# Gated transposing loads and a new step order in a fused attention and GELU kernel

## The chip, the cores and the metric

The kernel runs on one core of one Trainium2 chip. The metric is the device time of one execution in microseconds (us). A core has five engines that each work through their own list of instructions in order: TensorE (PE in the profile; PEld is its loading of weights), VectorE (DVE), ScalarE (ACT), GpSimd (POOL) and SyncE (SP). Transfers between the chip's main memory (DRAM) and the core are DMAs. An engine issues them, and they then run beside it; an instruction that needs the data waits for the landing.

## What is computed

The reference is a cross-covariance attention followed by a feed-forward layer with a tanh GELU. Cut to what matters:

```python
B, N, C = 4, 6080, 256                    # q, k, v: float32 [4, 6080, 256]
qn = q / norm(q over N);  kn = k / norm(k over N)
s = kn.transpose(0, 2, 1) @ qn / tau      # [4, 256, 256], one small matrix per batch
a = softmax(s over the last axis)
x = (v @ a).reshape(24320, 256)
h = x @ w_in                              # [24320, 2048]
g = 0.5 * h * (1 + tanh(sqrt(2 / pi) * (h + 0.044715 * h**3)))
out = g @ w_out                           # [24320, 256], float32
```

## The kernel before, in words

For each batch b the kernel folds the attention matrix into the first weight matrix: AW[b] = a @ w_in, of 256 by 2048. What is left per token is gelu(v @ AW[b]) @ w_out. The tokens of the four batches are cut into 25 blocks m = 0 to 24, of 1024 tokens in most cases, each in two halves t = 0 and 1 of 512 columns.

**Attention part.** q and k come in chunks of four rows of 128 tokens, cast to bf16 by DMAs that GpSimd issues (`load_one`, L243, steps `lq` and `lk`; four buffers each). TensorE adds up the matrix of k and q row by row (`gram_row`, L290, steps `r`, tile G), and the squares for the norms are made beside it (steps `z`, `d`, `f`). A short chain then makes AW of the next batch (`aw` and `ac` steps). Batch 0 is done ahead of everything else; batches 1 to 3 are spread among the blocks of the batch before.

**The v tiles.** A half block of v takes two DMAs. `cast_v` (L306, step `lv`, for instance `1:lv1` for block 1, half 1) lets GpSimd issue a load that casts 512 tokens from float32 to bf16 into a DRAM tile vb; there are five such buffers. `load_vt` (L319, step `lt`) lets SyncE issue a transposing DMA (DMA_TRANSPOSE) from vb into the tile vT, channels by tokens, with three buffers for whole blocks. The three first halves (block 0, and half 0 of block 1) are transposed by TensorE instead (steps `vp` and `vc`). SyncE also issues the output's stores (`store`, L771, steps `O`), four DMAs for each half block, in the same list.

**The block part.** The first product is done in two ways: plainly (steps `j`, L560, with the GELU in steps `J`) for some of the 16 feature groups, and for the others by a scheme with seven products in place of eight (steps `s..m1` to `s..m7`, L628, with sums of v tiles made by VectorE in steps `vs` and copies and GELUs around them). The second product is of the same kind (steps `M`, L739, of which TensorE has 1400 matmuls), with sums of g tiles by VectorE (steps `T`), and VectorE turns the result for the stores (steps `c11` to `c22`, L768).

**What sets the order.** All of this is one list, `ORDER` (from L962), of 4017 steps written out. A step's name is block:step or b-batch:step. The loop at the end of the kernel goes through it and issues each step's instructions, so that each engine gets its instructions in the order of this list; an engine waits only for the tiles that its next instruction needs.

**Gates.** `GATE[0]` (L518) always holds the last matmul that the list has issued in the steps `j`, `s..m`, `M` and `r`. `after(inst, gate)` (L92) makes an instruction wait for that matmul. Before the change, `step` and `block_step` (L895, L922) pass the gate to the cast loads alone: `lq`, `lk` and `lv`. Such a load is issued when TensorE has reached its place in the list. A transposing load has no gate: SyncE issues it as soon as its vb tile has landed, its vT buffer is free and what stands before it in SyncE's list is done.

Of the kernel before, what the change touches and what calls it, by code (L numbers as in the profile page):

```python
# [973 lines left out]
1:j21 2:lv1 1:s3m5 0:M5A b1:r1.2 1:vs1 2:lt0 b1:r1.3 1:s3y5 1:s4m1 1:s3m2 1:s3m6 1:J21 1:s4m5 b1:zk1
1:s3G0 0:M5B 1:s4y5 0:T2a 1:s3ap 0:T2b 1:s4cq b1:zq0 :pS4 0:M6A 1:s3m3 1:s4m2 1:s4m6 1:s4ap b1:r2.0
0:M6B 1:s3m7 1:s4G0 1:vs2 b1:r2.1 0:y5 1:s3G1 b1:r2.2 :pNA b1:lk4 1:j01 b1:zq1 1:s5m1 1:s4m3 0:ap
1:s4m7 1:s3ax 0:M7A 0:M3A 1:s3Gx 1:J01 0:T4a 0:M7B 1:s3m4 1:s4G1 1:s5cq b1:f1.1 b1:zq2 1:s4ax 1:s4m4
b1:r2.3 1:s4Gr 1:s5m5 0:M3B 1:s5m6 1:s3Gr b1:lq4 1:s5y5 1:s5m2 1:s6m5 1:s5G0 1:s4Gx b1:r3.0 b1:f0.1
1:s6m1 0:T4b 0:ax 0:c12 1:s5ap b1:f1.2 1:s6cq b1:dk2 0:M4A b1:r3.1 1:s5m7 1:j20 b1:r3.2 1:s5ax
1:s6y5 1:s5m3 b1:f2.1 b1:zk3 1:J20 1:s6m6 1:s6ap b1:lq5 1:s5G1 0:M4B 1:s5m4 b1:r3.3 0:c21 1:s7m5  # L980
1:s5Gx 1:s6m7 1:s6m2 1:s5Gr 1:s6ax 1:s7m1 1:s6G0 1:s7cq 1:s6m3 2:j00 1:s7y5 1:M1A 1:s6G1 1:s7m6
1:T3a b1:f1.3 b1:r4.0 1:s7ap 1:s6m4 b1:r4.1 2:J00 2:lt1 2:j20 b1:r4.2 1:s7m7 1:s7m2 1:s7m3 1:s6Gx
b1:lq8 0:O0 b1:zq3 3:lv1 1:T1a 2:J20 2:j10 1:s7G1 1:s7ax 1:M1B b1:f3.1 b1:lq7 1:T2a 2:J10 b1:dk4
1:s7m4 2:vs0 1:s7Gx 1:s7G0 1:s7Gr b1:r4.3 b1:r5.0 1:s6Gr b1:r5.1 1:M5A b1:r5.2 1:x1 2:j11 1:T3b
2:vs1 2:s2m1 1:T1b 2:j21 2:J11 2:J21 b1:zq4 b1:lk9 2:s2m5 1:M6A 1:M2A 1:M2B 2:s2cq b1:lq6 2:s2y5
b1:lk6 b1:zq5 2:s2m6 2:vs2 1:T2b 2:s2m2 2:s3m1 2:s2ap b1:lk7 1:M5B 2:s2m7 1:M6B b1:zk5 2:s2m3
b1:f3.2 2:s2G0 1:c11 4:lv1 1:y5 2:j01 3:lt0 2:s3cq 2:s2ax 3:lt1 2:s2m4 2:s2G1 1:ap 2:J01 2:s3m6
2:s3m2 2:s2Gr 2:s3m5 1:T4a 1:M3A b1:f5.1 2:s4m5 2:s3y5 2:s3G0 2:s4m1 2:s3ap b1:f3.3 0:c22 1:M3B
2:s4y5 2:s4cq b1:f3.4 2:s3m3 2:s3m7 b1:r5.3 2:s2Gx 2:s4m6 2:s3G1 2:s4m2 1:M7A 2:s4ap 2:s4G0 2:s3ax
b1:r6.0 2:s4m3 b1:r6.1 2:s5m5 2:s3m4 b1:zq6 1:T4b 2:j30 b1:lk8 2:s4G1 2:s3Gr b1:r6.2 3:j11 2:s3Gx  # L990
2:s4m7 2:s5y5 2:s5m1 1:M7B 1:c12 2:s4ax b1:r6.3 3:J11 2:s4m4 2:s5cq 2:J30 2:s6m1 2:s4Gr 2:s6cq
b1:r7.0 2:s4Gx 2:s5m2 b1:f4.1 1:ax 0:O1 b1:dk6 2:s5m6 1:M4A 2:s6m5 2:s5ap 2:s5G0 2:s5m7 b1:f5.2
5:lv0 2:s6y5 2:s6m2 2:s5ax 5:lv1 2:s5m3 2:s6m6 2:s6G0 1:M4B 1:c22 2:s5G1 2:j31 2:s5Gx b1:lq9 2:s7m1
2:s6ap 1:c21 2:s5m4 2:J31 b1:f5.3 2:s6m7 2:s5Gr 2:M1A 2:s7cq 2:T3a 2:s6m3 b1:f5.4 b1:zk7 b1:r7.1
2:s7m5 3:j30 2:s7m6 2:s6ax 2:M1B b1:r7.2 2:s6m4 b1:r7.3 2:s7y5 b1:lq11 2:s7ap 2:s6G1 3:J30 2:s6Gx
2:T1a 2:s7m7 2:s7m2 2:s7m3 3:j21 2:s7ax 2:x1 b1:f6.1 2:s6Gr b1:r8.0 2:M2A 2:s7m4 b1:r8.1 2:s7G1
3:J21 3:j00 2:T2a 2:s7G0 3:vs0 2:s7Gx 3:j01 b1:lk10 3:j10 b1:r8.2 b1:r8.3 2:s7Gr 2:T3b 3:s2m1 3:J01
b1:zq7 3:vs1 3:J10 2:M2B 3:s2cq 2:T1b 1:O1 2:M5A 3:s2m5 b1:lk11 3:J00 3:s2m2 3:s2y5 3:s2m6 3:s3m1
3:s2G0 b1:f7.1 2:M5B 2:M6A b1:zk9 3:s3cq 2:c11 3:vs2 3:s3m5 3:s2ap 2:y5 3:s3y5 3:s2m7 3:s2m3 b1:r9.0
2:T2b b1:lq10 3:s3m6 2:M6B 3:s2ax 3:s3ap 3:s2G1 b1:zq9 3:s2m4 3:j20 3:s2Gx 2:ap 2:T4a 3:s3m7 3:s3ax  # L1000
4:lt0 3:s3m2 3:s2Gr 3:s3m3 3:J20 3:s3G1 2:M7A 3:s4m1 3:s4cq 2:M3A 3:s3m4 3:s4m5 3:s3G0 3:s4m2 3:s3Gr
b1:f7.2 3:s4y5 2:M3B 3:s4G0 3:s5m1 b1:dk8 b1:r9.1 3:s4m6 2:T4b 3:s3Gx 5:lt0 2:c12 b2:lk0 5:lt1 3:j31
2:M7B 3:s5cq 3:s4ap 3:s4m7 3:J31 b1:f9.1 b1:f7.3 4:j10 b1:zq8 3:s5m2 3:s5m5 3:s5m6 4:J10 3:s4ax
3:s4m3 3:s4m4 3:s5G0 2:ax b1:f7.4 4:j00 3:s5y5 3:s5ap 2:M4A b1:r9.2 2:c22 4:J00 3:s4G1 3:s6m1 3:s4Gx
b1:f8.1 3:s5m3 b2:lq1 3:s6cq 3:s5m7 3:s5G1 3:s6m5 2:M4B 3:s6y5 3:s6m6 3:s4Gr b1:r9.3 3:s5ax 4:j30
2:c21 3:s5m4 b1:r10.0 3:s6m2 3:s6ap 3:s7m1 3:s6m7 b1:r10.1 3:s7m5 b1:r10.2 3:s6m3 b1:r10.3 3:s5Gx
4:J30 3:s6G0 b1:f9.2 3:s7cq 3:s6ax 4:lt1 3:s6m4 3:s7m2 3:s7y5 3:s7m6 4:j01 3:s6G1 3:s5Gr 3:s6Gr
3:T3a 4:j20 3:s7ap 4:j21 3:s7m3 3:T1a 3:s7m7 3:s6Gx 3:s7ax 3:M1A 4:J20 4:J21 3:T2a b1:f9.3 3:s7G0
b1:r11.0 3:s7m4 4:s3m1 b1:dk10 b1:r11.1 b1:r11.2 4:J01 3:s7G1 8:lv1 3:s7Gr 3:M1B b1:r11.3 4:s2m1
4:s3cq 3:x1 3:s7Gx 3:M5A 4:vs0 b1:gc b1:zq10 3:M6A b1:f9.4 4:s3m2 1:O0 4:vs1 4:s2m5 4:s2cq 4:s3G0  # L1010
6:lv1 4:s2y5 3:M2A 3:T3b 3:M2B 4:vs2 b1:zq11 6:lv0 4:s2m2 3:T1b 4:s3m5 3:c11 4:s2m6 4:s2G0 4:s3m6
4:s2ap 4:s3y5 3:M5B 3:y5 4:j31 3:T2b 4:J31 4:s4m5 4:s3ap 4:s2m3 4:s2m7 3:M6B 4:s2G1 4:s3m7 4:s2ax
4:s4m1 3:ap b1:zk11 b1:f10.1 4:s4cq b1:f11.1 2:O0 4:s3m3 4:s2m4 b1:f11.2 4:s3G1 4:s4y5 3:M3A 4:s4m2
4:s2Gx 4:s2Gr 4:s4m6 4:s4ap 3:M3B 4:s4G0 b1:f11.3 4:j11 4:s5m1 6:lt0 4:s4m3 2:O1 3:M7A 4:J11 4:s3ax
4:s4m7 b2:lq0 4:s5cq 3:c12 4:s5m2 4:s3m4 b2:lk2 b1:f11.4 4:s5m5 4:s5m6 4:s4G1 4:s3Gx b1:ss 4:s3Gr
4:s5y5 3:T4a 4:s4ax 4:s5G0 4:s6m1 3:M7B 4:s6cq 4:s4Gx 4:s6m5 b1:sv 4:s5ap 4:s6y5 4:s4m4 4:s6m6
4:s5m3 3:ax 4:s4Gr b1:pow 4:s6m2 4:s5G1 4:s5m7 5:j40 4:s6G0 3:M4A 4:s7m1 b1:kf 3:T4b 3:M4B 4:s6ap
b1:kr 4:s6m3 4:s5ax 3:c22 5:J40 4:s7cq 4:s7m5 b1:krp 4:s7m6 4:s6G1 4:s7y5 4:s5Gx 4:s5m4 4:M1A 3:c21
4:s6m7 5:j01 4:M1B 4:s5Gr b1:S0 4:s7m2 b1:S1 b1:th0 5:j41 5:j10 4:s7ap b1:th1 5:J01 6:lt1 4:T3a
5:j00 4:s7m3 4:s6ax b1:dn b2:lq2 4:s7m7 4:s7G0 5:J41 4:s6m4 3:O1 5:j30 4:s6Gx 4:T1a 5:j50 b1:rc3  # L1020
4:s7ax 5:J00 b1:rc2 b1:rc1 5:J10 4:s7G1 5:j11 4:M5A 4:s7m4 5:J50 4:x1 5:vs0 b1:rc0 5:s3m1 4:M2A
4:s6Gr 4:s7Gr 5:j31 5:J11 5:J30 5:J31 4:M2B 5:vs1 b1:eT 5:s3m5 5:s3cq 5:j21 5:j51 4:s7Gx 4:c11 5:J21
5:J51 5:s3m2 b1:aw4 5:s3y5 4:T2a 7:lv0 b1:aw6 b1:rsum b1:rs 5:s3G0 5:s3m6 4:M6A 4:T3b b1:ac6 b1:aw2
b1:aw3 5:s3ap b1:ac4 b1:aw0 4:T1b 5:vs2 b1:ac2 b1:ac3 b1:aw7 b1:ac0 5:s4m5 5:s3m3 5:s4m1 b1:ac7
# [269 lines left out]
```

## Time and profile before

| what | value |
|---|---|
| time of three runs | 694.0, 696.05 and 697.69 us; median 696.05 |
| the profiled execution's own time | 698.06 us |
| its span, from the first to the last instruction | 696.3 us |
| mean clock granted to TensorE | 0.987 of full speed |
| busy: PE, ACT, DVE | 667.8, 635.2 and 624.8 us |
| transposing loads (vT<-vb) | 47, median 5.4 us from issue to landing |
| cast loads of v (vb<-in_v_dram) | 37 of 256 KB in 4.9 us, and ten smaller ones |
| cast loads of q and k | 33 of 256 KB each in 5.9 and 6.8 us, and smaller ones |
| output stores | 160 of 128 KB in 3.4 us, and smaller ones |

How to read it: an engine's busy time is the time in which it executes at least one instruction; waits and the issuing of DMAs are not counted. A busy share is a mean over stages with different limits, so the waits and the single stretches tell more than the sums. For a DMA the profile gives the time from its issue to its landing. PEclk is the share of full clock that TensorE was granted. A line such as L560 is the line of the kernel that issued the instruction, and `vT<-vb` names the tile that is written and the one that is read.

### The profile page before, as it was taken

How to read it: one execution, taken by the hardware profiler on the slowest of the kernel's cores; microseconds unless marked ns; L12 is line 12 of the kernel's file. 1: busy time of each engine (PE TensorE's matmuls, PEld its weight loads, DVE VectorE, ACT ScalarE, POOL GpSimd, SP SyncE). 2: the span in 40 equal slices, each digit the busy share in tenths (PEclk: the TensorE clock that was granted, in tenths of full speed). 3: DMA queues.
4: the chain of work that ended last, by engine and by line, in shares of the span. 5: the costliest groups of instructions: out<-in, count | busy, mean ns of one | idle time of the engine just before them, and what ended most of it. 6: DMA issues, size and time to landing. Idle time of an engine off the chain costs nothing.

```text
span 696.3 us, 10272 instructions
## 1 busy us (share of the span) xinstructions
PE 667.8 (96%) x3471; PEld 335.3 (48%) x3471; DVE 624.8 (90%) x922; ACT 635.2 (91%) x1224; POOL 88.6 (13%) x163
## 2 busy tenths in 40 slices
...
PEclk9998899999999999999999999999999999999998
...
GB/s 240 207 262 111 114 136 150 171 96 99 128 58 125 123 123 131 177 44 117 138 77 76 117 167 139 129 121 64 102 90 57 52 115 67 73 20 126 31 40 110
DMA packets 165093, 78.80 MB, mean 113 GB/s; under 512 B 148992, under 2 KB 153472, under 8 KB 164320
## 3 DMA queue, kind: packets, MB, share of 16 engines
...
## 4 chain that ended last, share of the span: by engine, by line
PE 83%; DMA 10%; ACT 5%; issue 1%; DVE 0%; POOL 0%; POOLq 0%; DVEq 0%; ACTq 0%
PE u L739 21%; PE rb L628 15%; PE j L560 11%; PE p L739 11%; PE qb L628 8%; PE c L739 5%; PE G L296 4%; PE qa L628 4%; DMA vT<-vb 3%; DMA qk<-in_k_dram 3%; DMA k<-in_k_dram 2%; PE awp L501 2%; DMA vb<-in_v_dram 1%; DMA qk<-in_q_dram 1%; ACT g L572 1%; ACT g L653 1%
## 5 line engine op out<-in xcount | busy, mean ns | idle before, releaser
L739 PEld LDWEIGHTS <-wcomb 128*128 128x128 bf16 x1400 | 137.1, 98 | 145.8 <-issue 2.3
L739 PE MATMUL u<-t,wcomb 128*128 128x512 bf16 (+3 forms) x600 | 146.8, 368 | 0.0
L572 ACT ACTIVATE g<-j 128x512 bf16<-128x512 f32 (+1 forms) x204 | 123.6, 651 | 11.7 <-PE j L560 11.6
L560 PE MATMUL j<-vT,aw 128*128 128x512 bf16 (+2 forms) x456 | 125.2, 380 | 8.1 <-DMA vT<-vb 7.9
L648 DVE TENSOR_TENSOR qb<-rb,yw 128x512 f32<-128x512 f32 (+2 forms) x137 | 92.9, 680 | 13.4 <-PE rb L628 5.1
L628 PE MATMUL rb<-tv,sw 128*128 128x512 bf16 (+2 forms) x274 | 100.9, 375 | 0.0
L651 DVE TENSOR_TENSOR xw<-rb,yw 128x512 f32<-128x512 f32 (+2 forms) x137 | 91.6, 669 | 7.5 <-PE rb L628 5.9
L739 PE MATMUL p<-g,wcomb 128*128 128x512 bf16 (+3 forms) x400 | 96.7, 368 | 0.0
L662 ACT ACTIVATE g<-xw 128x512 bf16<-128x512 f32 (+2 forms) x137 | 90.8, 668 | 0.2
L653 ACT ACTIVATE g<-qa 128x512 bf16<-128x512 f32 (+2 forms) x137 | 86.0, 633 | 3.0 <-PE qa L628 2.6
L656 ACT ACTIVATE g<-qb 128x512 bf16<-128x512 f32 (+2 forms) x137 | 85.4, 627 | 3.1 <-PE qb L628 2.8
L646 ACT ACTIVATE yw<-qb 128x512 f32<-128x512 f32 (+2 forms) x137 | 85.9, 632 | 2.4 <-PE qb L628 2.0
L643 ACT ACTIVATE qa<-rb 128x512 f32<-128x512 f32 (+2 forms) x137 | 85.8, 629 | 2.0 <-PE rb L628 0.6
L659 ACT ACTIVATE g<-rb 128x512 bf16<-128x512 f32 (+2 forms) x137 | 85.0, 633 | 2.0 <-PE rb L628 2.0
L628 PEld LDWEIGHTS <-sw 128*128 128x128 bf16 x548 | 53.7, 98 | 56.5 <-issue 0.4
L560 PEld LDWEIGHTS <-aw 128*128 128x128 bf16 x456 | 44.7, 99 | 54.3 <-DMA vT<-vb 8.4
L628 PEld LDWEIGHTS <-aw 128*128 128x128 bf16 x411 | 40.5, 99 | 41.1 <-issue 0.5
L720 DVE TENSOR_TENSOR t<-g,g 128x2048 bf16<-128x2048 bf16 (+3 forms) x50 | 58.1, 1162 | 1.2 <-ACT g L569 0.6
L712 DVE TENSOR_TENSOR g<-g 128x2048 bf16<-128x2048 bf16 (+3 forms) x50 | 57.9, 1158 | 0.2
L718 DVE TENSOR_TENSOR t<-g,g 128x2048 bf16<-128x2048 bf16 (+3 forms) x50 | 57.8, 1159 | 0.2
L722 DVE TENSOR_TENSOR t<-t,g 128x2048 bf16<-128x2048 bf16 (+3 forms) x50 | 57.7, 1159 | 0.1
L309 POOL DMA_DIRECT2D vb<-in_v_dram x47 | 24.0, 511 | 259.2 <-PE rb L628 92.5
...
## 6 DMA issues: line engine op xcount, KB each, us to landing
out_dram<-ot SPq DMA_DIRECT2D x160, 128.0 KB, 3.4
...
wst<-in_moe_w_out_dram POOLq DMA_DIRECT2D x2, 1024.0 KB, 11.2
qk<-in_q_dram POOLq DMA_DIRECT2D x3, 512.0 KB, 14.4
...
```

Of the source, the lines that this page charges most:

```text
L560: GATE[0] = nc.tensor.matmul(hp[:, :n].rearrange("p (t x) -> p t x", t=2) if t == 2 else hp[:, :n], lhsT=AW[b][:, cc, fc * 128 : fc * 128 ...
L572: nc.scalar.activation(g[:, t, fc % 8, :hc], hp[:, :hc], AF.Gelu_apprx_tanh)
L628: GATE[0] = nc.tensor.matmul(acc[:, :hc], lhsT=lhs, rhs=rhs, start=i in (1, 5), stop=True, skip_group_check=True)
L643: nc.scalar.activation(Q0[m, p][:, :hc], RB[m, p][:, :hc], AF.Copy)
L646: nc.scalar.activation(YW[m, p][:, :hc], Q1[m, p][:, :hc], AF.Copy)
L648: nc.vector.tensor_add(Q1[m, p][:, :hc], RB[m, p][:, :hc], YW[m, p][:, :hc])
L651: nc.vector.tensor_add(XW[m, p][:, :hc], RB[m, p][:, :hc], YW.pop((m, p))[:, :hc])
L653: nc.scalar.activation(g[:, 0, e, :hc], Q0.pop((m, p))[:, :hc], AF.Gelu_apprx_tanh)
L656: nc.scalar.activation(g[:, 1, e, :hc], Q1.pop((m, p))[:, :hc], AF.Gelu_apprx_tanh)
L659: nc.scalar.activation(g[:, 0, e + 1, :hc], RB.pop((m, p))[:, :hc], AF.Gelu_apprx_tanh)
L662: nc.scalar.activation(g[:, 1, e + 1, :hc], XW.pop((m, p))[:, :hc], AF.Gelu_apprx_tanh)
L739: GATE[0] = nc.tensor.matmul(ACCS[m, acc][:, :hc], lhsT=wcomb[:, w, fc, :], rhs=x[:, fc, :], start=first and k_ == 0, stop=k_ == 3, skip_g ...
```

## The change

`load_vt` takes a gate as the cast loads do, and `block_step` passes `GATE[0]` to it. SyncE therefore issues a transposing load no earlier than TensorE has finished the matmul that stands before the load in the list. The list itself is replaced by another one with the same 4017 steps, in which the `lt` steps stand away from the `lv`, `lq` and `lk` steps. Nothing else changes: the same instructions on the same tiles.

```diff
-    def load_vt(m, t):
+    def load_vt(m, t, gate=None):
         hc = SB[m][2]
-        nc.sync.dma_start_transpose(out=vt(m)[:, t, :, :hc], in_=v_bf.pop((m, t))[:hc, :])
+        after(nc.sync.dma_start_transpose(out=vt(m)[:, t, :, :hc], in_=v_bf.pop((m, t))[:hc, :]), gate)
...
             elif what[:2] == "lt":
-                load_vt(m, int(what[2]))
+                load_vt(m, int(what[2]), GATE[0])
```

Of the list, the first lines stand here; the rest is changed in the same way up to its end:

```diff
-0:j00 b0:aw3 b0:ac3 b0:aw2 b0:ac2 b0:w00 0:j20 0:j10 1:lv1 0:J10 b0:aw4 b0:aw5 b0:ac4 b0:w01 b1:lq0
-b0:aw6 0:j50 0:J20 0:J00 b0:ac6 0:j60 0:j30 b0:aw7 b0:w12 b0:ac5 0:J50 0:s7m1 0:s6m1 0:vp1 b0:ac7
...
-0:j71 0:J61 b1:lq2 0:J71 1:lt1 0:j51 b1:lk5 0:j81 b0:w02 0:J81 0:M1A 0:ja0 0:s6G1 1:j40 0:s6Gx 0:J51
...
+0:j00 b1:lk0 b0:aw2 b0:aw3 0:j20 0:j10 b0:aw5 b0:ac2 b0:ac3 b0:aw4 0:j40 b0:aw6 b0:w00 0:j30 0:J20
+b0:ac5 b0:ac4 0:J00 b0:ac6 0:J40 1:lv1 0:vp1 0:ja0 0:vc10 0:s6m1 0:vc11 0:j70 0:j90 b0:aw7 0:J10
+1:lt1 0:J30 0:j80 0:Ja0 0:j01 b0:w12 0:vs0 b1:lq0 0:s6cq b0:ac7 0:J70 0:ja1 b0:w02 0:j81 0:J90 1:vp0
```

The loads and the steps that read them first, as they follow each other in the two lists around block 1's second half and around blocks 8 and 9 (other steps left out):

```
before: 1:lv1 b1:lq0 b1:lq3 b1:lk0 b1:lq1 b1:lk1 b1:lk2 2:lv0 b1:lq2 1:lt1 b1:lk5 8:lv0 4:lv0 1:j51
after:  b1:lk0 1:lv1 1:lt1 b1:lq0 2:lv1 b1:lq1 b1:lk1 8:lv0 b1:lq2 1:j21 b1:lk3 3:lv0 b1:lk2
before: b2:lq4 9:lv1 b2:lk4 b2:lq5 b2:lq6 b2:lk6 9:lt0 8:lt0 10:lv1 b2:lq7 b2:lk7 b2:lq9 8:j10 b2:lk9
after:  b2:lk5 b2:lq4 b2:lk4 b2:lq5 b2:lk6 8:lt0 9:lt0 b2:lq6 9:lv1 b2:lq7 13:lv1 8:j30 b2:lq8 10:lv1
```

More of the change, by code (lines that the diff above doesn't have):

```diff
@@ L974 @@
[L974 to L1024, printed above, removed]
-5:s4cq 5:s3m7 4:T2b 4:M5B 5:s4y5 b1:aw5 5:s4m6 5:s4m2 5:s3ax 4:y5 4:M6B 5:s4G0 5:s3m4 5:s4ap 5:s4m3
@@ L1055 @@
-8:s2m1 6:c21 8:j11 7:s6Gr 7:s7m4 b2:lk9 7:M1A b2:f5.1 8:j30 8:J20 b2:r6.0 8:s2cq 8:vs0 b2:lk8 8:s2m2
-7:s7Gr 7:s7Gx 8:J11 7:T2a 8:j00 8:vs1 b2:r6.1 8:J30 8:s2G0 12:lv1 9:lt1 8:s2m5 8:s2m6 7:M1B 8:s2y5
-b2:lq8 b2:r6.2 b2:r6.3 8:j21 7:x1 b2:f4.1 8:j31 8:vs2 8:J00 b2:dk6 7:M2A b2:r7.0 b2:f5.2 8:s2ap
-8:s3m5 8:s2m3 8:J21 6:O1 8:J31 8:s3m1 7:T3b 8:s2m7 7:M2B b2:zq6 7:T4a 8:s2G1 8:s2ax 7:M6A 8:s3y5
-7:T1b 7:c11 8:s3cq 8:s3m6 8:s2m4 8:s3m2 7:M5A 8:s4m1 b2:zk7 7:T2b 8:s3G0 8:s2Gr 7:M5B 7:M6B b2:lk11
-8:s4cq 8:s3ap b2:f6.1 8:s2Gx 7:y5 8:s4m5 7:ap b2:f5.3 8:s3m3 b2:lq11 8:s3m7 8:s3ax b2:zq7 10:lt0
@@ L1085 @@
-15:lv1 10:s2Gx 9:M6B 13:lt1 b2:S0 10:s3G1 10:s4cq 10:s4m2 10:s4m6 b2:S1 10:s3ax 10:s4y5 10:s3m4
-b2:th1 9:ap b2:th0 10:s4ap 8:c22 10:j21 9:M3A 10:s3Gx 8:O1 10:s2Gr 9:M3B 9:T4b 10:s5m1 10:s3Gr
-10:s4G0 10:s4m7 9:c12 b2:dn 11:j31 10:s4ax 10:s5cq 10:s4m3 b2:rc0 9:M7A 10:s6m1 b2:rc3 10:s4G1
-10:s5m5 10:s5m6 11:J31 10:J21 10:s6m5 10:s5m2 10:s5y5 10:s5ap 10:s6cq 9:M7B 9:ax 10:s4m4 13:lt0
-10:s6m6 10:s5m7 10:s6y5 10:s5m3 10:s6m2 9:M4A 10:s4Gx 10:s6ap 10:s5G0 10:s6m3 10:s7m1 10:s4Gr
-10:s6G0 10:s5ax 10:s7m5 b2:rc2 11:j01 10:s6m7 10:s5G1 b2:rc1 9:M4B 10:s5Gx 11:J01 10:s7cq 10:s6ax
@@ L1161 @@
-16:J31 16:j21 16:J00 16:s2cq 16:j30 b3:f11.3 15:T3b 16:s2m6 16:s2m2 b3:f11.4 15:M2B 16:s2y5 15:T2a
-16:J21 16:s3m1 16:s2ap 15:T1b 16:J30 16:J20 b3:ss 16:s2m7 16:s2G0 16:s2m3 16:s3cq 16:s3m5 16:s3m2
-16:s2G1 b3:sv 16:s2ax 16:s3G0 b3:pow 20:lv1 15:M6A 16:vs2 16:s3y5 16:s3m6 15:T2b 16:s4m1 16:s2m4
-15:M5A 17:lt0 b3:kf 15:M5B 16:s2Gx 16:s4cq 16:s2Gr 16:s4m2 16:s3ap 15:c11 15:T4b 16:s5m1 16:s3m7
-b3:kr 16:s4G0 b3:krp 15:y5 16:s3m3 b3:S0 17:lt1 15:M6B 16:s5cq b3:S1 16:s4m5 16:s4m6 16:s3ax 16:s3G1
-b3:th0 16:s4y5 16:s5m5 16:s5m6 15:ap 16:s3m4 16:s4ap 16:s5m2 16:s5y5 15:M3A 19:lv0 14:O1 16:s4m7
@@ new lines @@
+b0:ac5 b0:ac4 0:J00 b0:ac6 0:J40 1:lv1 0:vp1 0:ja0 0:vc10 0:s6m1 0:vc11 0:j70 0:j90 b0:aw7 0:J10
+1:lt1 0:J30 0:j80 0:Ja0 0:j01 b0:w12 0:vs0 b1:lq0 0:s6cq b0:ac7 0:J70 0:ja1 b0:w02 0:j81 0:J90 1:vp0
+0:J80 b0:w10 0:vs1 0:s6m2 0:J01 0:j21 b0:w11 0:Ja1 0:J81 0:j31 1:vc00 0:s6m5 0:s6G0 0:j11 0:J21
+0:vs2 1:vc01 0:jb1 :pA11 2:lv1 0:j51 0:J31 0:j91 b1:lq1 0:s6y5 0:j50 0:s6m6 :pS3 0:Jb1 0:J11 0:J91
+0:J50 :pA12 0:J51 :pF0 0:j71 0:j41 0:j60 0:j61 0:s6ap 0:J61 1:j00 0:J60 0:s7m1 b0:w13 0:s6m7 :pF1
+0:s6ax 0:J71 1:j30 0:M1A 1:J00 1:J30 0:s7m5 1:j50 0:s6m3 0:J41 0:jb0 0:s7y5 b1:lk1 0:T3a 0:M1B
@@ new lines @@
+b1:lq4 1:s4cq 1:vs2 1:s4m2 0:y5 b1:r2.3 1:s3m3 1:s3m7 0:T4b b1:r3.0 b1:zk1 1:s4y5 1:s3G1 1:s4m6
+1:s4G0 0:ap b1:r3.1 1:s3ax b1:lk5 0:M3A 1:s4ap b1:f0.1 1:s3m4 1:s3Gx 1:s5m1 0:T4a 1:s4m7 0:M3B
+1:s5cq 1:s3Gr b1:zq2 1:s5m2 1:s4ax 0:M7A 1:s5m5 1:s4m3 1:s5G0 1:s4Gx 0:c12 b1:r3.2 1:s5m6 1:s5y5
+b1:f1.1 b1:dk4 1:s4m4 1:j20 1:s6m1 0:M7B 1:s4G1 1:s4Gr 1:J20 2:lt1 1:s5ap 1:s6cq 1:s5m3 1:s5m7
+1:s7m1 b1:r3.3 b1:f1.2 1:s6m5 b1:r4.0 2:lt0 1:s6m2 0:ax 1:s5G1 1:s6m6 b1:r4.1 1:s5ax 1:s6y5 1:s5m4
+1:s6G0 1:s5Gx b1:dk2 0:M4A 1:s6ap 1:s6m7 1:s7m5 b1:f2.1 1:s7cq b1:r4.2 1:s6ax 1:s5Gr b1:zq3 1:T3a
@@ new lines @@
+1:s6m3 0:M4B 1:s7y5 0:c21 b1:r4.3 1:s7m6 1:s6m4 1:s6Gx 1:M1A 1:s7m2 1:s6G1 1:s7ap 2:j11 1:s7m7
+1:s7m3 b1:lq8 1:M1B 1:T1a 1:s7ax 2:j21 1:s6Gr b1:lq6 1:s7G0 b1:zq4 1:T2a 1:s7m4 1:s7G1 b1:lk6 2:vs0
+1:x1 2:j00 b1:lk7 1:s7Gr 0:c22 b1:r5.0 2:j10 1:s7Gx 2:s2m1 2:J21 3:lv1 2:vs1 1:T3b b1:lq7 2:J00
+1:M2A 2:J10 2:J11 1:M2B 2:j01 1:c11 2:s2cq 2:j30 2:j20 2:s2m5 2:s2m2 2:J01 2:s2m6 2:J30 2:J20 2:s3m1
+1:T1b 2:s2G0 1:M6A 1:M5A 0:O1 1:T2b 2:s2y5 2:s3cq 2:s2ap 2:s3m5 b1:zk3 2:s3y5 2:s3m6 2:s2m7 2:s2m3
+2:s2G1 2:s3m2 b1:f1.3 2:vs2 1:M5B 2:s2ax b1:f3.1 2:s3G0 2:s4m1 2:s2m4 1:y5 2:s4cq 1:M6B 2:s3ap
@@ new lines @@
+2:s2Gr 2:s3m7 2:s4m2 b1:zk5 b1:f3.2 1:ap b1:r5.1 2:s4m6 3:lt1 b1:r5.2 b1:r5.3 2:s4m5 1:T4b b1:f3.3
+1:M7A 2:s4G0 2:s2Gx 2:s4y5 1:M7B 2:s3ax b1:zq5 2:s3Gx 2:s5m5 b1:r6.0 2:s4ap 2:s3m3 2:s3G1 2:s3m4
+b1:f3.4 2:s3Gr b1:f5.1 2:s4m3 2:s4G1 1:M3A 3:lt0 2:s5m1 2:s4m7 2:s5cq 1:M3B 2:s5m2 1:T4a b1:r6.1
+2:s5m6 2:s5y5 b1:zq6 1:ax 2:s5G0 1:M4A 2:s4ax 3:j11 0:O0 b1:f4.1 2:s5ap 2:s4Gx 3:j31 1:c12 3:J11
+2:s5m7 2:s5m3 2:s6m1 3:J31 b1:r6.2 2:s5G1 1:M4B b1:dk6 2:s6cq 5:lv0 2:s5ax b1:f5.2 1:c21 2:s6m5
+2:s5m4 2:s6m2 b1:f5.3 2:s6m6 b1:lk8 2:s5Gx 2:s7m1 2:s4m4 2:j31 4:lv1 2:s6y5 2:s6ap 2:s6G0 2:s5Gr
@@ new lines @@
+3:s2G1 b1:dk8 2:M6B 3:s3m5 3:s3y5 3:j10 3:s3m6 3:s2ax 3:s2m4 1:O1 2:ap b1:f7.1 3:s3ap 3:s2Gx 2:T4a
+2:M3A 4:lt0 3:J10 3:s4m1 3:s2Gr 2:T4b 2:M3B b1:zq9 3:s3m7 3:s3ax 3:s4m5 3:s4cq 3:s4y5 b1:zk9 2:c12
+2:M7A 3:s4m2 3:s3m3 b1:r8.3 3:s4m6 2:M7B 3:s4ap 3:s4G0 3:s3G1 3:s5m5 4:lt1 3:s3m4 2:ax 3:s4m3 3:s3Gx
+3:s3Gr 3:s5m1 3:s4m7 2:M4A b1:r9.0 3:s5cq 3:s5m2 3:s5m6 b1:f7.2 3:s6m1 2:M4B 3:s4ax b1:f7.3 3:s4G1
+3:s5y5 3:s5G0 3:s4m4 b1:f9.1 3:s6m5 3:s4Gx 3:s6cq b1:r9.1 3:s5ap 3:s5m7 3:s4Gr 5:lt0 3:s6m2 3:s6m6
@@ new lines @@
+b1:f7.4 3:s7m1 3:s5m3 b1:r9.2 2:c21 4:j30 3:s5ax b1:r9.3 3:s6y5 3:s6ap 2:c22 3:s6G0 3:s6m3 b1:r10.0
+3:s5G1 3:s5Gx 3:s6m7 3:s7cq 3:s5m4 4:J30 b1:f8.1 3:s7m5 3:s7y5 b1:r10.1 b1:dk10 b1:r10.2 3:s6ax
+3:s6G1 3:s7m6 3:s7m2 4:j01 3:s6m4 3:s7G0 4:j21 3:s7ap 4:j31 3:s7m7 b1:r10.3 3:T3a b1:r11.0 3:s6Gx
+3:s5Gr 3:s7ax 3:T1a b1:r11.1 b2:lq2 4:J01 b1:r11.2 3:s7m3 4:j00 8:lv1 4:J31 4:s2m1 3:s7m4 3:s6Gr
+3:s7Gx b1:r11.3 3:s7G1 4:j20 b1:f9.2 2:O0 3:M1A 4:s3m1 4:vs0 6:lv1 4:J00 4:J20 4:J21 3:T3b 3:M1B
+b1:gc 4:s2m5 4:vs1 4:s2cq 3:s7Gr 3:x1 4:j10 4:s2y5 b2:lk2 b1:f9.3 b1:zq10 3:T1b 3:T2a 4:s2m6 4:s2m2
@@ new lines @@
+4:s5m7 4:s5ax 4:s6m5 4:s4m4 4:s5G1 b1:ss 4:s6y5 5:j00 b1:sv 3:c22 b1:pow 4:s4Gr 4:s6G0 4:s5m4 4:s6ap
+3:O1 b1:kf 4:s7m1 3:M4A 3:M4B 4:s6m7 4:s5Gx 4:s6m3 5:J00 4:s7cq 4:T3a b1:kr 4:s7m6 4:s5Gr 4:s7m5
+4:s6ax 4:s7y5 3:c21 4:s7m2 4:s6Gx b1:krp 6:lt1 4:s7ap 5:j01 b1:S0 4:s6m4 4:s7G0 4:M1A 4:s7m7 b1:S1
+5:J01 4:s7ax 5:j51 5:j50 4:T1a b1:th0 b1:th1 4:s6G1 b1:dn 4:s6Gr 5:j31 4:M1B b1:rc1 4:s7m4 4:s7m3
+5:J31 b1:rc3 b1:rc0 5:j41 b1:rc2 6:lt0 4:M5A 5:vs0 4:s7Gr 5:j21 5:J51 4:x1 5:j10 5:J50 4:s7G1 b1:eT
@@ new lines @@
+5:s4Gx 5:s6m2 5:s4m4 b2:lk3 5:s5ap 5:s6G0 b1:w00 b1:w01 5:s4Gr 6:j40 5:s6m5 5:s6y5 5:s6m6 5:s5m7
+b1:w02 6:j41 5:s5m3 b2:lk1 4:M7B 6:J40 5:s7m1 5:j20 5:s6ap 5:s5ax 7:lv1 4:ax 5:s5G1 6:J41 5:s7cq
+5:s6m7 5:s6m3 5:s7m5 5:s7m6 5:s5m4 4:M4A 4:c22 5:s7m2 5:s5Gx 5:s7y5 5:s6G1 5:J20 6:j20 5:s6ax 6:j01
+5:s7ap 5:s7m7 5:s7G0 4:O1 b1:w03 5:s6Gx 6:J01 6:J20 5:s6m4 4:M4B 5:T3a 5:s7ax 6:j50 5:s6Gr 6:s3m1
+5:s5Gr 5:s7m4 6:s3cq 4:c21 5:s7m3 6:j11 6:s4m1 5:s7G1 5:T1a 6:vs0 6:J11 b1:w13 6:vs1 5:M1A 6:s3m2
+5:s7Gr 5:s7Gx 5:M1B 6:J50 5:T3b 6:j51 6:j21 6:s3G0 7:lt1 5:M5A 5:x1 5:T1b 6:J51 4:O0 3:O0 6:J21
```

470 lines of the change are left out of this document (248 added, 222 removed).

## The prediction

> **What bounds the kernel now.** I read the page's busy rows first, then TensorE's waits, the table by stage, the chain of waits around the two stretches that stand out, and last the DMA views. From the page:
>
> ```profile
> PE 667.8 (96%) x3471; PEld 335.3 (48%) x3471; DVE 624.8 (90%) x922; ACT 635.2 (91%) x1224; POOL 88.6 (13%) x163
> ...
> PEclk9998899999999999999999999999999999999998
> ```
>
> TensorE (PE) leads; its clock dips in two places. Its waits after the start are two, both for DMAs:
>
> ```profile
> PE j L560 <- DMA vT<-vb: 7.9, 1, 7.9
> PE G L296 <- DMA k<-in_k_dram: 2.3, 1, 2.3
> ```
>
> By stage (stretch, its length, then busy time and count per engine; last PEclk, DMA share, GB/s):
>
> ```profile
> 64.00:68.00 4.00, 0.00 (x0) 0.00 (x0) 0.00 (x0) 0.00 (x0) 0.00 (x0) 0.50 0.83 111
> 68.00:72.00 4.00, 3.62 (x9) 1.34 (x10) 1.83 (x2) 1.19 (x2) 0.00 (x0) 0.50 1.16 146
> 72.00:76.00 4.00, 4.00 (x17) 1.78 (x16) 3.29 (x4) 2.36 (x5) 1.55 (x3) 0.73 0.77 142
> 256.00:260.00 4.00, 4.00 (x19) 2.10 (x17) 2.26 (x4) 2.74 (x6) 0.00 (x0) 0.69 1.12 185
> 80.00:230.00 150.00, 150.00 (x754) 73.34 (x752) 146.31 (x219) 149.59 (x288) 20.64 (x38) 1.00 0.75 116
> 262.00:680.00 418.00, 418.00 (x2074) 202.31 (x2072) 396.62 (x574) 404.54 (x801) 35.22 (x65) 1.00 0.59 95
> ```
>
> Between 80 and 230 and between 262 and 680 us TensorE never rests, at full clock; each wait is followed by some microseconds at half clock. "Busy" alone does not prove peak, so I took the matmul spacing: the chain shows four matmuls of 512 columns in 0.86 us, 0.216 each. At that rate the order's matmuls (products 287.3, "small" 202.6, j 96.9, gram 31.1, aw 13.0, rest 2.2) sum to 633.1 us. TensorE runs them from 37.8 to 689.9, 652.1 us: 19 us more. About 4 of these lie in short float32 matmuls and issue gaps, which stay. The other 15 lie at the two waits, which the chain (start, length, what) shows:
>
> ```profile
> 40.46 9.44 DMA vb<-in_v_dram
> 49.91 18.42 DMA vT<-vb
> 68.38 1.89 PE j L560 x4
> ...
> 238.59 15.96 DMA k<-in_k_dram
> 254.60 0.38 PE G L296 x2
> ```
>
> First place: the matmul before ends at 60.3 and the next starts at 68.38, 8.0 us lost; then work worth 3.2 us takes from 68.38 to 74.5 at half clock, 2.9 lost: 10.9. Second place: 252.15 to 254.60, 2.45 lost, and 1.65 more until 258.6 at half clock: 4.1. Together **15.0 us**.
>
> **Why these loads are late.** A v tile is cast to a DRAM tile by GpSimd's queue (lv), then read transposed by SyncE's (lt). All transposing loads, issue to landing:
>
> ```profile
> DMA to landing us min/median/max: 2.7/5.4/19.2
> ```
>
> Alone they take 3.2 (at 80.9, 164.5, 371.8); the one that stalls TensorE takes 18.4, with casts issued at 51.1 to 59.1 beside it, and at 237.6 one takes 19.2 beside casts issued from 235.8 to 251.5, of which the awaited k load takes 16.0. What moved then: casts alone (42 to 48 us), stores alone (233 to 236), and transposing loads mixed with casts (60 to 68):
>
> ```profile
> DMA packets 913, 1.88 MB, mean 313 GB/s; under 512 B 50, under 2 KB 562, under 8 KB 898
> ...
> DMA packets 2246, 0.56 MB, mean 186 GB/s; under 512 B 2246, under 2 KB 2246, under 8 KB 2246
> ...
> DMA packets 490, 0.78 MB, mean 98 GB/s; under 512 B 290, under 2 KB 290, under 8 KB 468
> ```
>
> Apart they run at 313 and 186 GB/s, mixed at 98 with the engines still marked busy. Mixing is what hurts. [...]
>
> **The change, part by part.**
>
> *The order.* The steps are the same 4017, so the work is the same. To compare orders I give each step a "place": 37.8 plus the TensorE time of all matmul steps before it. In the kernel before this fits issue times (place 39.96, issued 40.46; 50.55, issued 51.07). Of the 47 lt steps, 32 have a cast within 4 us of place in the old order, one in the new: 1:lt1. All others have at least 4.75 us since the last cast and 4.3 to the next. A cast beside no transposing load lands in about 4.1 (q at 90.7), a load alone in 3.2 to 3.8, so pairs meet rarely.
>
> Second place: the old order has lt at 229.8, 234.4 and 249.9 among fourteen casts from 222.7 to 251.2. The new one has casts up to 225.1, lt at 233.1 and 234.2, casts again from 240.2: **-4.1 us**; the next deadline there is 8:lt0's first reader, at 244.3. The casts that move closest to their readers are b1:lk1 (55.5 to 61.6, 6.05 us ahead) and b1:lk2 (7.6 ahead); against 4.1 alone that costs 0, and with the collision of the first place open it belongs to rival B.
>
> First place: the one exception. 1:lv1 is issued at about 42.6 as second cast behind the w_out staging; the second one before (q at 41.0) landed 10.1 later, at 51.1. So 1:lt1 starts at 51.1, its gate (44.5) long open, while three casts (0.25 MB each, last issued at 50.2) are in flight; the next comes at 56.0. Nearest rows: 5.9, 6.1 and 9.9 with two or three beside it (451.8, 398.2, 430.2), 18.4 with six issued after it. I take 6: lands at 57.1; its first reader 1:j21 is at place 57.5, about 58.0 on the clock. No stall: **-10.9**, with 0 to 11 us of it at risk.
>
> *The gate.* 47 waits on SyncE. A wait that is already met costs 17 ns there (SPq EVENT_SEMAPHORE, min and median), under work that nobody awaits. TensorE gives such signals already for 119 cast loads without a gap in 568 us: 0. Behind a gated load SyncE's queue holds output stores (0:O0 is turned at 82 and now waits behind 3:lt0, gated at 101.8); by the places one of the three output buffers is free before each turn, so 0, and at worst one store's 5 us now and then, which shows as a DVE wait. The gate also takes lead away: loads now start at their place, 6.5 to 8.4 us ahead of their first reader for eight of them (2:lt1 6.5, 3:lt1 7.1, 7:lt1 7.2). Alone they need 3.2 to 3.8: 0 (rival D).
>
> *Hand-overs between engines.* Every ScalarE and VectorE step moves with the rest. Before, TensorE waits for neither after 38 us, though both are 95 to 100% busy; the new order keeps similar distances (median ScalarE copy to its matmul 1.08 in both). Not below 0, as there is no such wait to lose; up to 3 us. I take 0.5.
>
> *The end.* 23:O0 moves ahead of 24:O0, whose turn is still tied to the last matmul. Last landings now are 694.57 and 694.74 (23:O0) after 694.41: -0.3, between -0.5 and 0.
>
> **Sum**, against the profiled execution (698.06 us, span 696.3): 698.06 - 4.1 - 10.9 + 0.5 - 0.3 = 683.3; I say 683.0. The median before, 696.05, is 2.0 lower than that execution; as the sum removes the parts that may vary, I keep 683 and let the median's distance set the low end, 680.5.
>
> **Rivals.**
>
> A, the forecast (60%): both waits go: 680.5 to 686.5.
>
> B (14%), the first load still collides, as in the rows of 9.9 to 11.1 (11.1 at 422.6): lands at 61 to 62, TensorE waits 3 to 4 us, then 1.6 to 2.9 at half clock: 688 to 690. For it: 1:lt1 is the one load that is not apart. [...]
>
> C (11%), it doesn't do what it says: mixing is not the cause but what the DMAs ask at that time, so loads stay as late (18.4 from 51.1 gives 69.5, 11.5 late, 2.9 at half clock, 14.4 in place of 10.9): 698.06 + 3.5 - 4.1 = 697.5 with the second place mended, 698 with nothing changed, and as low as 694 by the spread of the runs before. [...] Against it: 98 GB/s in the mix against 313 apart.
>
> D (15%), slower: the gate's lost lead. Eight loads now start 6.5 to 8.4 (mean 7.6) us ahead of their reader, where before SyncE issued them when the cast landed. If they land as those beside casts or stores at 168.6, 236.1 and 422.6 (10.7, 9.0, 11.1: mean 10.3), each is 2.7 late plus 1.6 at half clock: 8 x 4.3 = 34, so 683 + 34 = 717. It decides where the eight together cost 15, 1.9 each (0.7 late, 1.2 at half clock), a landing after about 8.3 us, against the median of 5.4.
>
> A measurement can tell about 0.5% (3.5 us) from no change. Faster by more: A and B, 0.74; within: C, 0.11; slower: D, 0.15. The range 680.5 to 695 holds A, B and half of C, about 0.8.
>
> **What would show it.** Right: no "PE j <- DMA vT<-vb" and no "PE G <- DMA k" wait above 1 us; PEclk at 9 from the second slice on; transposing loads with a maximum below 11 us and a median near 4. Wrong: the first load landing after 58 (B, C); several waits of 2 to 4 us on vT, each with a clock dip (D); TensorE waiting for DVE or ACT, which would be the new order's hand-overs.

## The result, and the profile after

| | before | after |
|---|---|---|
| median, same chip | 696.05 us (7 runs, 693.5 to 699.3) | 691.0 us (7 runs, 689.8 to 691.3) |
| ratio | | 0.9926, 95% interval 0.9899 to 0.9952 |
| profiled execution, span | 698.06, 696.3 us | 690.03, 688.3 us |
| end of TensorE's list, then to the end of the span | 689.8, 6.5 us | 683.1, 5.2 us |
| transposing loads, median and longest to landing | 5.4, 19.2 us | 3.1, 5.3 us |

The kernel became faster by 5 us, where 13 were forecast. Both waits of before are gone, as forecast, and a new one took half of their place. The page of after (61 of the 3471 matmul records are missing from this trace; the weight loads are complete):

```profile
PE 663.0 (96%) x3410; PEld 334.4 (49%) x3471; DVE 625.6 (91%) x922; ACT 635.1 (92%) x1224; POOL 88.2 (13%) x163
...
PEclk9999999999999999999999998999999999999999
```

The clock has one dip, in a slice that had none before. TensorE's and VectorE's waits in after (what waits, for what; total, times, longest):

```profile
PE rb L628 <- DVE xw L651: 4.1, 1, 4.1
```

```profile
DVE ot L768 <- DMA out_dram<-ot: 6.8, 2, 5.6
```

After the start there is no wait of TensorE for vT and none for k. All transposing loads, issue to landing:

```profile
DMA to landing us min/median/max: 2.5/3.1/5.3
```

But TensorE now waits once, for 4.1 us, for VectorE, and VectorE, in its turn of an output tile (L768), waits for a store to free an output buffer. By stage:

```profile
64.00:68.00 4.00, 3.95 (x20) 1.93 (x20) 4.00 (x6) 4.00 (x8) 1.57 (x3) 1.00 1.11 215
68.00:72.00 4.00, 4.00 (x26) 2.38 (x25) 3.49 (x7) 4.00 (x7) 1.07 (x2) 1.00 0.93 170
...
416.00:420.00 4.00, 3.74 (x18) 1.58 (x17) 0.90 (x2) 2.47 (x5) 0.00 (x0) 1.00 1.07 205
420.00:424.00 4.00, 0.20 (x1) 0.10 (x1) 1.54 (x3) 0.22 (x1) 0.00 (x0) 0.74 0.24 44
424.00:428.00 4.00, 3.87 (x13) 1.72 (x12) 3.97 (x5) 4.00 (x8) 0.00 (x0) 0.50 0.00 0
```

From 64 to 72 us, where TensorE stood before, it works at full clock. From 419.6 to 423.8 it stands (4.2 us lost), and the matmuls up to 428.7 run at half clock (2.5 more): 6.7 us. VectorE is the first to rest (0.90 of 4 us busy from 416). The chain of waits of after (start, length, what) says for what:

```profile
405.18 0.32 SPq L782
...
406.72 15.62 DMA out_dram<-ot
...
422.36 0.05 DVEq L768
...
422.46 0.72 DVE ot L768
```

This is the store 12:O1 (block 12, second half): four DMAs issued from 405.18 to 406.72, the last landed at 422.34. Its half block took 17.2 us, where a store with no cast load beside it takes 4.7 in the median (24 half blocks of after). Ten cast loads were issued from 402.9 to 414.8. The DMA queues while it waits (404 to 423 us; packets, MB, share of the engines' time), and in the eight microseconds of the worst crowding (413 to 421 us):

```profile
q0 software_dynamic: 1216, 2.61, 78.4%
q1 hardware_dynamic: 2112, 0.52, 15.3%
```

```profile
q0 software_dynamic: 586, 1.45, 92.8%
q1 hardware_dynamic: 497, 0.12, 10.4%
```

q0 carries GpSimd's cast loads and q1 SyncE's stores and transposing loads. From 413 to 421 both move about as many packets (586 and 497). Of the casts' packets 461 are of 2 KB and 32 of 15 to 16 KB, and 479 of the store's are of 256 bytes, so the store moves 0.12 MB against 1.45. With so like a number of packets, the queue with the small ones got a twelfth of the bytes of the other; how the engines choose between the two queues no run here shows.

### The profile page after: what moved, and what is told of

Read it like the earlier page. It is cut to its first block, busy times and chain, and to the rows that moved or that the text cites. A ratio compares the mean times of both kernels' runs of the same rounds, so it can differ in the third digit from the quotient of the medians.

```text
span 688.3 us, 10199 instructions
## 1 busy us (share of the span) xinstructions
PE 663.0 (96%) x3410; PEld 334.4 (49%) x3471; DVE 625.6 (91%) x922; ACT 635.1 (92%) x1224; POOL 88.2 (13%) x163
## 4 chain that ended last, share of the span: by engine, by line
PE 86%; DMA 6%; ACT 5%; DVE 1%; issue 1%; SPq 0%; POOL 0%; DVEq 0%; POOLq 0%
PE u L739 22%; PE rb L628 16%; PE j L560 13%; PE p L739 12%; PE qb L628 8%; PE c L739 5%; PE G L296 4%; PE qa L628 4%; DMA qk<-in_k_dram 2%; DMA out_dram<-ot 2%; PE awp L501 2%; DMA qk<-in_q_dram 1%; ACT g L572 1%; ACT g L662 1%; ACT qa L643 1%
## 5 line engine op out<-in xcount | busy, mean ns | idle before, releaser
L739 PE MATMUL u<-t,wcomb 128*128 128x512 bf16 (+3 forms) x583 | 143.3, 368 | 0.8
L572 ACT ACTIVATE g<-j 128x512 bf16<-128x512 f32 (+1 forms) x204 | 122.0, 661 | 2.5 <-PE j L560 2.5
L628 PE MATMUL rb<-tv,sw 128*128 128x512 bf16 (+2 forms) x269 | 97.6, 375 | 0.6 <-DVE qb L648 0.2
L662 ACT ACTIVATE g<-xw 128x512 bf16<-128x512 f32 (+2 forms) x137 | 92.8, 680 | 5.6 <-DVE xw L651 5.6
L646 ACT ACTIVATE yw<-qb 128x512 f32<-128x512 f32 (+2 forms) x137 | 87.6, 645 | 2.4 <-PE qb L628 2.2
L643 ACT ACTIVATE qa<-rb 128x512 f32<-128x512 f32 (+2 forms) x137 | 87.8, 643 | 2.2 <-PE rb L628 1.6
L653 ACT ACTIVATE g<-qa 128x512 bf16<-128x512 f32 (+2 forms) x137 | 87.6, 648 | 1.6 <-PE qa L628 1.3
L656 ACT ACTIVATE g<-qb 128x512 bf16<-128x512 f32 (+2 forms) x137 | 87.6, 644 | 1.5 <-PE qb L628 1.2
L659 ACT ACTIVATE g<-rb 128x512 bf16<-128x512 f32 (+2 forms) x137 | 87.2, 647 | 0.8 <-PE rb L628 0.6
L628 PEld LDWEIGHTS <-sw 128*128 128x128 bf16 x548 | 53.8, 98 | 56.4 <-issue 1.7
L628 PE MATMUL rb<-tv,aw 128*128 128x512 bf16 (+2 forms) x137 | 51.1, 376 | 4.3 <-DVE xw L651 4.1
```

Of the source, the lines that this page charges most:

```text
L572: nc.scalar.activation(g[:, t, fc % 8, :hc], hp[:, :hc], AF.Gelu_apprx_tanh)
L628: GATE[0] = nc.tensor.matmul(acc[:, :hc], lhsT=lhs, rhs=rhs, start=i in (1, 5), stop=True, skip_group_check=True)
L643: nc.scalar.activation(Q0[m, p][:, :hc], RB[m, p][:, :hc], AF.Copy)
L646: nc.scalar.activation(YW[m, p][:, :hc], Q1[m, p][:, :hc], AF.Copy)
L653: nc.scalar.activation(g[:, 0, e, :hc], Q0.pop((m, p))[:, :hc], AF.Gelu_apprx_tanh)
L656: nc.scalar.activation(g[:, 1, e, :hc], Q1.pop((m, p))[:, :hc], AF.Gelu_apprx_tanh)
```

## The experiments

Two theories stood against each other for the missing 8 us. **S**: a store among cast loads is slow, the turn waits for its buffer, TensorE for the turn. **R**: something else is late at that place.

**One store earlier (e2).** In the changed kernel the store 11:O1 (block 11, second half) has its last tile turned at 385.9 us, but stands in SyncE's list behind the gated load 16:lt0 and is issued at 428.1. When block 13 asks for an output buffer at 416.9, one of the three is held by 11:O1 and one by 12:O0, which is stored later still, so the only one that can come free is that of 12:O1.

```diff
-13:s4y5 13:s5G0 15:lt0 13:s5m5
+13:s4y5 13:s5G0 15:lt0 11:O1 13:s5m5
...
-14:s4G1 b3:f5.4 11:O1 14:s5m5 15:lt1
+14:s4G1 b3:f5.4 14:s5m5 15:lt1
```

> The changed kernel with one step moved: the store 11:O1, whose tile was turned at 381 us, stands behind 15:lt0 (394 us by the list) and not behind 16:lt0 (423 us); nothing else differs. Theory S (slow store): the forecast missed by the one new stall at 419 to 428 us, where VectorE's turn of block 13 waits 5.6 us for an output buffer whose store 12:O1 took 17.2 us beside ten cast loads, and TensorE loses 4.2 us of wait and about 3 us of half clock behind it. With 11:O1 early, block 13 gets that buffer instead, its store has landed by about 404 us, and the wait of 5.6 us on VectorE goes although 12:O1 still takes some 17 us: 690.0 - 7.2 = 682.8 us, between 682 and 685. Rival R (the turn is not what holds TensorE, something else is late at the same place): the wait of VectorE on the store goes but TensorE stands as long for another engine or load: 689 to 691 us.

Measured: 683.2 us (682.8 to 683.7); ratio to before 0.9816 [0.9784, 0.9847]. The wait of 5.6 us is gone although 12:O1 took 18.2; the one row of VectorE for a store that is left lies at 258 us:

```profile
DVE ot L768 <- DMA out_dram<-ot: 2.1, 1, 2.1
```

The same stage of this kernel, VectorE 3.97 and 3.99 of 4 us busy in place of 0.90 and 1.54:

```profile
416.00:420.00 4.00, 4.00 (x20) 1.84 (x19) 3.97 (x7) 4.00 (x9) 0.04 (x1) 1.00 1.06 204
420.00:424.00 4.00, 3.95 (x23) 2.05 (x22) 3.99 (x5) 4.00 (x9) 0.00 (x0) 1.00 0.76 129
```

So the turn and its buffer were what held TensorE; R falls.

**The casts later, the store where it is (e5).** Is the store slow because of the casts, or because of its place in SyncE's queue?

```diff
-13:M2B 13:T2a b3:f5.2
+13:M2B 13:T2a b3:lk8 b3:lq8 17:lv1 18:lv0 b3:lk9 b3:lq9 b3:f5.2
```

(The six steps are taken out of their old places. In the changed kernel they were issued from 404.2 to 414.8 us, here from 417.5 to 420.1.)

> The changed kernel with six of the ten cast loads that lay beside the store 12:O1 (b3:lk8, b3:lq8, 17:lv1, 18:lv0, b3:lk9, b3:lq9) put behind 13:T2a, 9 us after the store's place; the store and its place in the queue of SyncE are unchanged. Theory S: the store is slow because cast loads share the DMA engines with it, so with four left beside it it takes 7 to 11 us as stores beside four or five casts do in both traces, not 17.2; it lands before block 13 asks for the buffer at 416.7 us, and the time is 682 to 685 us. Rival Q (the store is late by its place behind other work of SyncE's queue, or a store of this size takes that long whatever lies beside it): 15 us or more again, the 5.6 us wait on VectorE stays, 689 to 691 us.

Measured: 683.6 us (683.3 to 684.2). The store's DMAs took at most 6.2 us each, in place of 15.6, and the half block 7.7 with the four casts that were left:

```profile
DMA to landing us min/median/max: 2.4/4.5/6.2
```

With the same place in the queue and fewer casts the store is fast: the casts beside it are the cause.

**The order alone (e3) and the wait alone (e4).** Each is one half of the change: the changed kernel with `load_vt(m, int(what[2]))` again, and the kernel before with the gate.

```diff
-                load_vt(m, int(what[2]), GATE[0])
+                load_vt(m, int(what[2]))
```

> The new order without the wait: the transposing loads start when their cast has landed and their buffer is free, as before the change. Theory T (what counts is the distance in time between transposing and cast loads, and both parts are needed for it): some of the 47 loads start earlier than their place, beside casts, so several land in 6 to 19 us again where all took at most 5.3; the stall at 419 us stays, as the store that it waits for is slow either way; 691 to 700 us. Rival O (the order does it all and the gate is idle): no landing over 6 us, 689 to 691 us.

> The old order with the wait alone. Theory T: the old places were not made for it. By the list of before, 32 of 47 transposing loads have a cast within 4 us of their place, and six have 6 us or less from their place to their first reader (0.65, 2.8, 3.5, 4.5, 6.0, 6.05 us), where a load took 5.4 us in the median: at least 4.8 + 2.6 + 1.9 + 0.9 = 10 us of waits and 2 to 3 us of half clock behind each of four, with both places of before (60 and 250 us) left as they are: 705 to 725 us. Rival G (the gate is what helps): 686 to 692 us.

Measured: the order alone 692.2 us (ratio 0.9953 [0.9929, 0.9976], not to be told from both together); the wait alone 707.7 (1.0178 [1.0140, 1.0216]). The order alone loses TensorE 5.5 us at the same store:

```profile
PE rb L628 <- DVE xw L651: 5.5, 1, 5.5
```

Its transposing loads take up to 15.7 us again, and none is awaited. So theory T is right that the loads mix again without the wait, and wrong that the wait is needed. With the wait alone, TensorE waits six times for a transposing load:

```profile
PE j L560 <- DMA vT<-vb: 13.4, 6, 6.9
```

The longest wait of before is still there (6.9). Of the other five, one is for a load that took 16.4 us among five casts; the other four loads took 3.0 to 6.4 us and were issued too close to their reader.

**The order alone with the store mended (e7).** To see whether the wait has a worth apart from that stall: e2 without the gate.

```diff
-                load_vt(m, int(what[2]), GATE[0])
+                load_vt(m, int(what[2]))
...
+13:s4y5 13:s5G0 15:lt0 11:O1 13:s5m5
```

> The changed kernel with 11:O1 early (683.2 us with the wait), and without the wait of the transposing loads. The order without the wait took 692.2 us, 1.2 more than both together, and its only long wait of TensorE was that for the store at 420 us, 5.5 us in place of 4.1. Theory O (the order does all the work here, and the 1.2 us was only a longer store): no wait of TensorE on a load although several transposing loads take 6 to 16 us, 682.5 to 684 us. Rival G (the wait has a worth of its own apart from that stall): 684.3 us or more, with TensorE or VectorE late behind a transposing load.

Measured: 683.6 us (683.4 to 684.6), against 683.2 with the wait. The landings are those of a mixture, and nobody waits for them:

```profile
DMA to landing us min/median/max: 2.6/3.7/15.5
```

In the new order the wait brings no gain that can be measured; the list does the work.

**The first place mixed again (e6).** Rival C of the prediction, that mixing costs nothing, tested in the changed kernel:

```diff
-0:J31 0:j91 b1:lq1 0:s6y5 0:j50
+0:J31 0:j91 b1:lq1 b1:lk1 8:lv0 b1:lq2 b1:lk3 0:s6y5 0:j50
```

(The four are taken out of their places. In the changed kernel they were issued from 56.0 to 59.0 us, here from 50.6 to 52.2.)

> The changed kernel with four cast loads (b1:lk1, 8:lv0, b1:lq2, b1:lk3) put back right behind b1:lq1, so that they are issued at some 50 to 52 us, beside the transposing load 1:lt1 (51 us), as four were in the kernel before; the wait and all else as changed. Theory T (a transposing load among cast loads is what is slow): 1:lt1 lands after 15 to 19 us instead of 5.3, at 66 to 70 us; its reader 1:j21 stands at 58, so TensorE waits 8 to 12 us and runs some 3 us at half clock: 701 to 705 us. Rival C (mixing costs nothing; the first place went because its load or its readers moved): 1:lt1 lands in 5 to 7 us, no wait: 689 to 691 us.

Measured: 699.7 us (697.8 to 702.8), 8.7 above the changed kernel, which ran on another chip; the ratio to before on the same chip is 1.0060 [1.0030, 1.0089], where the changed kernel had 0.9926. 1:lt1 was issued at 51.06, as without the four casts (51.14), and landed at 65.73, after 14.7 us in place of 5.3. The wait of before is back:

```profile
PE j L560 <- DMA vT<-vb: 8.0, 1, 8.0
```

Four 256 KB loads moved by some 6 us cost 9 us. The median is 1.3 below the expected range. The profiled execution, from which the landing and the wait are read, took 701.5 and lies in it, with the wait at the range's lower end.

**The first place alone (e9).** The kernel before, with six casts moved:

```diff
-b0:w03 0:s7m7 1:j10 0:T3a
+b0:w03 0:s7m7 1:j10 b1:lk1 b1:lk2 2:lv0 b1:lq2 b1:lq3 b1:lk5 0:T3a
```

> The kernel before (no wait, old order) with six cast loads (b1:lk1, b1:lk2, 2:lv0, b1:lq2, b1:lq3, b1:lk5) put behind 1:j10, 3 us after the first transposing load 1:lt1, and nothing else changed. Theory T: 1:lt1 lands at 55 to 57 us in place of 68.3, the first place's 8.05 us of wait and 2.85 of half clock go, the second place stays: 696.05 - 10.9 = 685.2, between 684 and 688 us. Rival: another wait takes most of that place (the casts that were moved are late for the Gram rows from 63 us on): 690 to 696 us.

Measured: 684.1 us (683.0 to 687.8), ratio 0.9846 [0.9808, 0.9884]. The median is 10.9 below that of before on the same chip (694.97), which is what the first place was worth. 1:lt1 landed at 54.3 and nobody waited for it. In the profiled execution TensorE's list ended 13.3 us earlier, though, 2.4 more: the second place's wait has shrunk to 0.3 us as well, though the loads there still mix (a transposing load at 249.6 took 17.5):

```profile
PE G L296 <- DMA k<-in_k_dram: 0.3, 1, 0.3
```

The load that is awaited there, b2:lk4, is the same in both kernels, and in both TensorE was ready for it 13.7 us after its issue. Before it landed after 16.0 us, here after 14.0. Six steps moved by hand, with no gate, do more than the whole change did.

**The slow store from another queue (e10, e11).** The changed kernel with 12:O1 alone issued by ScalarE, and by GpSimd:

```diff
+            elif (m, tj) == (12, 1):
+                eng = nc.scalar
```

> The changed kernel with the one slow store, 12:O1, issued by ScalarE in place of SyncE; its place, its casts and all else as they are. Theory P (the store shares the DMA engines packet by packet with the cast loads, and its 256-byte packets get little of them whichever queue they stand in): 14 us or more to landing again, and the stall at 419 us stays at 3 to 6 us; 689 to 692 us. Rival N (the store is slow because it stands in SyncE's queue): it lands in 5 to 8 us, the wait of VectorE goes, 683 to 685 us. ScalarE may stand 1 to 2 us for the turn ahead of the store in either.

> The same with 12:O1 issued by GpSimd, so that the store stands in one queue with the cast loads, behind those issued ahead of it and ahead of the later ones. Theory P (what is slow is a queue of small packets taking turns with a queue of large ones; in one queue there are no turns): it lands in 6 to 10 us like the casts around it, the stall goes, and the casts behind it are 1 to 3 us later: 683 to 686 us. Rival B (any store beside so many casts takes that long, since the engines are simply full): 14 us or more, 689 to 692 us.

Measured: 686.5 us from ScalarE (two runs), 683.6 from GpSimd (two runs). Issue to landing of the four DMAs, from ScalarE and then from GpSimd:

```profile
DMA to landing us min/median/max: 5.4/12.1/12.7
```

```profile
DMA to landing us min/median/max: 5.1/5.5/6.0
```

From ScalarE the half block went through another queue (q10: 2112 packets and 0.52 MB from 406 to 422 us, as many as q1 moved in after from 404 to 423) and took 14.1 us against 17.2 from SyncE, so it is not SyncE's queue. But the time was in neither theory's range: it landed 1.7 us earlier, VectorE waited 2.0 us in place of 5.6, no half clock followed, and some 1.1 us were lost at 408 instead, where ScalarE was late. From GpSimd it landed as fast as theory P said. Two things differ in that run, the queue and the size of the packets: the store moved in 128 packets of 4 KB, not 2048 of 256 bytes. Which of the two helps was not separated. That the queues take turns packet by packet, as theory P has it, was the author's assumption; no run shows it.

**Both stores early (e8).** A small stall of the same kind was left at 258 us, where VectorE waits for an output buffer 1.2 us in after and 2.1 in e2.

```diff
-6:s7m4 7:vs0 5:O1 7:J21
+6:s7m4 7:vs0 5:O1 5:O0 7:J21
...
-7:T1b 7:T2b 5:O0 7:M2A
+7:T1b 7:T2b 7:M2A
```

(11:O1 stands as in e2.)

> The changed kernel with 11:O1 early (683.2 us) and the store 5:O0, turned at 216 us and standing at 254, put right behind 5:O1 (219 us). At 257.4 to 259.5 us VectorE's turn of block 7 waits 2.1 us for a store that took 11.9 us beside six cast loads, and TensorE 1.4 to 1.6 us behind it. Theory S: block 7 gets the buffer of 5:O0 instead, and that wait goes: 681.5 to 682.2 us. Rival: another operand is as late there, 683.0 to 683.5 us.

Measured: 682.0 us (681.7 to 682.1), ratio to before 0.9805 [0.9781, 0.9830]: 13 us faster than before, and the best of all. VectorE waits for no store any more, and the clock has no dip:

```profile
PEclk9999999999999999999999999999999999999999
```

## Why the prediction was right and wrong, point by point

- **First place, -10.9: right.** 1:lt1 landed at 56.4 (forecast 57.1) after 5.3 us (forecast 6), and its reader did not wait. e6 brings the loss back with four casts, e9 takes it away in the old order.
- **Second place, -4.1: gone as forecast.** In the new list b2:lk4 is issued with no transposing load beside it and lands after 5.4 us, where it took 16.0. But the loss hung on a small margin: in e9 the loads there still mix, the same load takes 14.0, and only 0.3 us of the wait of 2.3 is left.
- **Hand-overs, +0.5: close, by a guess.** The prediction had no row for it and chose 0.5 between 0 and 3. TensorE's list ends 6.7 us earlier; the two places give 15.0, the waits for buffers take 6.7 and 1.1, which leaves +0.5. Of this TensorE's rows show 0.3 (it waits 0.5 us for aw at the start of the blocks, and 0.2 before); the rest was not located.
- **The end, -0.3: too small.** From the end of TensorE's list to the end of the span it was 6.5 us and is now 5.2: -1.3. The prediction took away one landing and left the next as it was. The last stores land faster too: the very last after 1.8 us, where it took 2.9.
- **The gate: the step that failed.** It said that "by the places one of the three output buffers is free before each turn, so 0, and at worst one store's 5 us". It was +7.8 (6.7 and 1.1). The places were right: 12:O1 was issued in time, and with a landing of 5 us it would have freed its buffer some 5 us before the turn asked for it. The landing was the error. The prediction had shown that transposing loads are late among casts (18.4 us against 3.2), and asked of each transposing load what lies beside it. It did not ask the same of the stores, which go through the same queue in packets of the same size (q1, 256 bytes), though the trace of before has stores of 21 and 16 us beside twelve and nine casts. Its row of 186 GB/s, set against the mixture as what the small packets do apart, was itself one of stores alone (2246 packets for 0.56 MB). The sign that it named for a wrong hand-over, TensorE waiting for VectorE, came, but from this wait: VectorE was itself waiting for a DMA. The heading was wrong too: without the gate (e3) the stall is there as well. It is the new list that bunches ten casts between two groups of transposing loads, puts a store among them, and leaves 11:O1 late.
- **The sum.** 698.06 - 15.0 + 0.5 - 1.3 + 7.8 = 690.1, against 690.03 profiled; as the 0.5 is what was left over, this sum has to close. The test is the last term: without it the sum is 682.3, and e8, which moves two stores to take that term away, has 681.8 in its profiled execution.
- **Rivals.** B did not come: the one load that was not apart took 5.3 us. C falls with e6, 14.7 against 5.3 us. Transposing alone is not what made a load slow here: the loads of after with no cast in flight took 3.1 us in the median, where a cast of q with no transposing load beside it took 4.1 (at 90.7 us of before). D did not come: no load took over 5.3 us, so a lead of 6.5 was enough. Loads with no cast in flight took 2.5 to 5.0 us (42 loads), a wider band than the 3.2 to 3.8 of the prediction. D's mechanism is real, though. In the old list, where leads are shorter, the gate alone costs 12 us (e4); 5.5 of them are further waits of TensorE for transposing loads.

What stays open: why the same mixture at the second place took 2 us less in e9, and whether the queue or the packets saved the store in e11.
